# K and V loaded as 8 KB rows on every fourth partition, in the forward and backward pass of one decode step

## The chip, the cores and the metric

The kernel runs on one core of a Trainium2 chip. The metric is device time in microseconds (us) for one execution; lower is better. Before the change three runs took 282.91, 283.11 and 283.65 us; the median is 283.11 us.

## The reference, cut to what matters

One token of each of four sequences (B = 4, model width D = 512) goes through a layer norm and then through two branches side by side: attention with a cache of keys and values (32 query heads, 8 key/value heads, head width Dh = 128) and a gated feed-forward network (F = 1792). The kernel returns the output and the gradients of all inputs but `B_x`.

```python
W = min(4096, max(256, Sk // 4))                  # 1024 of the 4096 cached positions
q = (xn @ wq).reshape(B, 1, 32, 128)...
k = repeat(k_cache[:, :, Sk - W:, :], 4, axis=1)  # v likewise
p = softmax(q @ k^T * Dh**-0.5);  o = p @ v
out = x + o @ wo + (gelu(xn @ w_gate) * (xn @ w_up)) @ w_down
# and jax.vjp of it: gradients of x, k_cache, v_cache, wq, wo, w_gate, w_up, w_down
```

The gradients of the caches have the caches' full shape, (4, 8, 4096, 128) in bf16. Their first 3072 positions are zeros, and these zeros have to be written: 50 MB of the 81 MB that the kernel writes.

## The kernel before, in words

**Order of the work.** First the feed-forward branch (to about 60 us), then the query and its incoming gradient, then one round of the attention loop for each sequence `b`, then the end: `dwo` and `dwq`, the gradients of the two projection matrices.

**Loads of K and V.** `load_kv` (the issue is L233) fetches one sequence's K or V, 2 MB, into a tile `[128, G, J, Dh]` with J = 8: partition p holds the eight positions 8p to 8p + 7 of every head, so one row is 8 x 128 x 2 bytes = 2 KB. It issues two transfers of 1 MB, for four heads each. The first K load goes through SP's queue (q1 of the profile), the other seven loads through Pool's (q0). K has two tiles in turn, `ka` and `kb`; V has one, `va`, so V of the next sequence is issued only when `odq(0, b)` has read the present one, and K of the sequence after the next when `odq(1, b)` has read its tile.

**One round of the loop.** `scores(0, b)` is Q K^T and `scores(1, b)` is dO V^T, where dO is the gradient that comes into the attention's output. In both, DVE turns the tile in 32 x 32 blocks of bf16 pairs (`t32`, L93, four instructions of 1024 pairs), and PE multiplies what it wrote with `bd`, the query or dO spread out over blocks (`sc_ps`, 32 matmuls a call). `softmax` makes `E_f`, its sum, `P_b` (bf16) and `P_f` (fp32). `turned` brings `P_b` with its keys onto the partitions: 32 matmuls of 32 columns with the selector `selp` into `pT_ps`, and one eviction, `pT`. `odq(0, b)` multiplies `pT` with V. `dvdk(0, b)` makes the gradient of V: PE writes `kv_ps`, ACT and DVE evict it (L88, L89) into two of the four `stg` buffers of 1 MB, and two transfers (L106) store them. `softmax_d` makes `dS_b`, which goes the same way through `turned`, `odq(1, b)` and `dvdk(1, b)`.

**Queues.** SP's queue is in program order and carries the 32 stores of zeros, 1.5 MB each, with at most three in flight. Most are held by a load or a result: two or three follow the landing of each V or K load. Pool's queue carries the loads of K and V and the stores of results. A scheduler that goes by its own estimate of times puts the instructions of PE, DVE, ACT and Pool in order; loads have high priority. On each engine instructions then run strictly in that order. In the kernel before, the scheduler puts `va` of the third sequence, `kb` of the fourth and `va` of the fourth on Pool each ahead of one or two stores whose data are ready sooner.

Of the kernel before, what the change touches and what calls it, by code (L numbers as in the profile page):

```python
# [8 lines left out]
ACT = mybir.ActivationFunctionType  # L9
ALU = mybir.AluOpType  # L10
AX = mybir.AxisListType
FP32 = mybir.dt.float32
# [6 lines left out]
def kernel(  # L19
# [84 lines left out]
    def store(eng, out, in_, kind, apart, **kw):  # L104

        d = eng.dma_start(out=out, in_=in_, **kw)  # L106
        for k in apart:
            tc.declare_no_dep(d.ins, group=k, reason="stores write disjoint parts of the outputs")
        tc.add_to_no_dep_group(kind, d.ins)
        return d  # L110

    def result(out, in_):
        return store(nc.gpsimd, out, in_, "rest", ["zeros", "rest"], single_packet=True)

# [45 lines left out]
    def mask(name, n, in_):  # L160
# [9 lines left out]
    hm = mask("hm", Q, ident_f[:].rearrange("p (h d) -> p h d", d=4))  # L170
    omt = const.tile([P, NQ, 2], FP32, name="omt")
    TT(out=omt[:], in0=gmask[:].rearrange("p (c g) -> p c g", g=2), in1=bm[:].unsqueeze(2).broadcast_to([P, NQ, 2]),
       op=ALU.mult)
    om = mask("om", 2, omt[:].rearrange("p c g -> p g c"))
    oms = const.tile([P, 2], FP32, name="oms")
    TS(out=oms[:], in0=om[:], scalar1=scale, scalar2=None, op0=ALU.mult)
    gmask_b = const.tile([P, G], BF16, name="gmask_b")
# [34 lines left out]
    t32(dyP, pairs(dy_b[:]), 256)  # L212
    dyBD = const.tile([P, NPB, 2, P], BF16, name="dyBD")
    nc.gpsimd.memset(dyBD[:], 0.0)
    dyPb = dyP.bitcast(BF16).rearrange("p n (x r) -> p n r x", r=2)
# [11 lines left out]
    def load_kv(b, k, pool, tag, eng, **kw):  # L227
        d_, src = ((k_t, A_k_cache), (v_t, A_v_cache))[k]
        tl = pool.tile([P, G, J, Dh], BF16, name=tag, tag=tag)
        for hf in range(2):  # L230
            hs = slice(hf * G // 2, (hf + 1) * G // 2)
            with tc.high_priority():
                d = eng.dma_start(out=tl[:, hs].rearrange("p g j d -> p g (j d)"),  # L233
                                  in_=src[b, hs, K0:Sk, :].rearrange("g (m j) d -> m g (j d)", j=J), **kw)
        d_[b] = tl
        return d
# [23 lines left out]
    if True:  # L260
# [85 lines left out]
        for wi, (wsb, dh, og) in enumerate(((wu_sb, dhu, out_7), (wg_sb, dhg, out_6))):  # L346
# [26 lines left out]
            for h in range(2):  # L373
                stg = stg_tile()
                for ci in range(2):
                    for a, q in enumerate(quad):
                        ps = bank("dwg_ps", "w", (P, FQ))
                        mm(ps[:], xn_b[q, 2 * h + ci:D:C], dh_f[q, :], pos=(Q * a, 0))
                        o_ = (ci * NQ + a) * FQ
                        evac(stg[:, o_:o_ + FQ], ps[:], FQ)  # L380
                result(dwg_v[h], stg[:, 0:2 * F])
        nc.vector.tensor_copy(out=dxf[:], in_=dxf_ps[:])
    ffn_open.__exit__(None, None, None)

    with tc.tile_pool(name="mid", bufs=1, reuse_waits="tile") as mid:
# [4 lines left out]
        with tc.tile_pool(name="att", bufs=1, reuse_waits="tile") as att:  # L390
            zeros(2, load_kv(0, 1, att, "va", nc.gpsimd, single_packet=True))
            zeros(3, load_kv(1, 0, att, "kb", nc.gpsimd, single_packet=True))


# [3 lines left out]
            for k in range(2):  # L398
                bd.append([])
                for u in range(2):  # L400
                    t_ = att.tile([P, DPB, NQ, 2, 2, Q], BF16, name=f"bd{k}{u}")
                    nc.gpsimd.memset(t_[:], 0.0)
                    bd[k].append(t_)
            selh = att.tile([P, P + 4], FP32, name="selh")
# [61 lines left out]
            def get_d(ps, u):  # L466
                l_ = dsc[:, 512:640] if u == 0 else dsc[:, 640:768]
                mm(ps[:].rearrange("p b d -> p (b d)"), l_, dM.rearrange("p b e k -> p (b e k)"))

            spread_rows(1, get_d)  # L470

# [9 lines left out]
            def scores(k, b):  # L481

                t_ = bd[k][b % 2]
                ps = bank("sc_ps", ("S", "dP")[k], (P, NJ))
                src = pairs((k_t, v_t)[k][b][:])
                for g2 in range(2):
                    for e in range(2):
                        sc = scratch()
                        t32(sc[:].rearrange("p (c j m) -> p c j m", c=NQ, j=J), src[:, g2:G:2, :, e * Q:(e + 1) * Q], 1024)
                        sb = sc[:].bitcast(BF16).rearrange("p (c n r) -> p c r n", c=NQ, r=2)  # L490
                        for r in range(2):
                            for c, q in enumerate(quad):
# [26 lines left out]
            def softmax(S):  # L519
# [17 lines left out]
                rr = small("rr")  # L537
                nc.vector.reciprocal(out=rr[:], in_=es_ps[:])
                P_b = att.tile([P, NJ], BF16, name="P_b", tag="P_b")
                nc.scalar.activation(out=P_b[:], in_=E_f[:], func=ACT.Copy, scale=rr[:, 0:1])  # L540
                P_f = att.tile([P, NJ], FP32, name="P_f", tag="P_f")
                p_done = nc.scalar.activation(out=P_f[:], in_=E_f[:], func=ACT.Copy, scale=rr[:, 0:1])
                load["act"] += 1400
                return P_f, P_b, p_done

            def softmax_d(P_f, dP):
# [11 lines left out]
                return dS_b  # L558

# [17 lines left out]
            def odq(k, b, pT):  # L577
# [45 lines left out]
            for b in range(B):  # L623
                S = scores(0, b)
                if b + 1 < B:
                    dP = scores(1, b)
                    refill(0, b + 1)
                    refill(1, b + 1)
                P_f, P_b, p_done = softmax(S)
# [10 lines left out]
                dvdk(0, b, spread(P_b, 0), rows[1])  # L640
                dS_b = softmax_d(P_f, dP)
                dST = turned(dS_b, 1)
                o_done = odq(1, b, dST)
# [134 lines left out]
```

## Time and profile before

| | |
|---|---|
| the profiled execution | 282.91 us, of which the span of the profile is 280.8 us |
| median of the runs | 283.11 us |
| PE, DVE, ACT, POOL busy | 67%, 58%, 44%, 21% of the span |
| moved by DMA | 112.2 MB at 400 GB/s on average |
| q1 (SP's queue) | 66.46 MB: zeros, weights, the first K |
| q0 (Pool's queue) | 45.35 MB: results 30.7 MB, K and V 14.7 MB |
| granted PE clock, mean | 0.58 of full speed |

A profile is of one execution. Busy shares are over the whole span, and what a stage waits for is read from that stage. In the names of groups, L117 is the helper that issues nearly all matmuls, so that tiles (`pT_ps`, `sc_ps`, `kv_ps`, `od_ps`) tell them apart. The DMA share is the mean busy share of the core's 16 DMA engines, and the modelled records can bring it a little over 1.

### The profile page before, as it was taken

What the parts mean: (1) busy time and instruction counts of PE and PEld (TensorE: products, weight loads), DVE (VectorE), ACT (ScalarE), POOL (GpSimd) and SP (SyncE); (2) the same over time, 40 slices, a digit from 0 to 9 for tenths busy, and PEclk for the clock granted to TensorE, in tenths of its full rate; (3) what the DMA queues carried; (4) which work ended last, traced back from release to release, by engine and by line L of the source; (5) the groups of instructions that cost most, each with busy time, mean ns of one, the idle gap of its engine ahead of it and who ended that gap; (6) DMA issues with size and microseconds to landing.
All of it is one profiled execution on the core that took longest, in us unless ns stands there. A gap on an engine that the chain in (4) does not pass through costs nothing.

```text
span 280.8 us, 4407 instructions
## 1 busy us (share of the span) xinstructions
PE 187.0 (67%) x1733; PEld 76.1 (27%) x1733; DVE 162.9 (58%) x309; ACT 124.3 (44%) x245; POOL 60.2 (21%) x135
## 2 busy tenths in 40 slices
PE   0318899859444899659956642963357998955870
PEld 0102354233122623224321321321034232511210
DVE  2879656898796525545128350474496104397870
ACT  1133764730100569634824402722441768445870
POOL 8500110169083314130040060020020020201110
PEclk9975955558955556655555555555555555685555
DMA  7999999999999999999999999999999999999995
GB/s 246 427 443 443 388 396 420 425 426 411 389 427 434 420 356 403 308 373 415 424 412 407 421 427 409 371 428 427 436 373 418 415 408 402 390 411 386 414 412 242
DMA packets 17027, 112.21 MB, mean 400 GB/s; under 512 B 1384, under 2 KB 1648, under 8 KB 11376
## 3 DMA queue, kind: packets, MB, share of 16 engines
q1 hardware_dynamic: 6688, 66.46, 57.0%
q0 software_dynamic: 10176, 45.35, 41.5%
q8 instruction: 13, 0.21, 0.3%
q10 hardware_dynamic: 144, 0.13, 0.1%
q14 instruction: 6, 0.05, 0.0%
HBM read 30.93 MB, written 81.01 MB: 399 GB/s over the span
## 4 chain that ended last, share of the span: by engine, by line
PE 25%; DMA 24%; DVE 13%; issue 4%; ACT 4%; POOL 1%; POOLq 0%; DVEq 0%; ACTq 0%
DMA out_dram<-stg 16%; PE kv_ps L117 9%; DVE scr L93 6%; DMA ka<-in_A_k_cache_dram 5%; PE sc_ps L117 3%; ACT stg L88 3%; DMA kb<-in_A_k_cache_dram 3%; PE od_ps L117 3%; PE ok_ps L117 2%; PE ob_ps L117 2%; DVE stg L89 2%; DVE wq_sb L93 2%; PE dxq_ps L117 2%; PE dwq_ps L117 1%; PE dwo_ps L117 1%
## 5 line engine op out<-in xcount | busy, mean ns | idle before, releaser
L88 ACT CAST stg<-kv_ps 128x512 bf16<-128x512 f32 x118 | 63.7, 606 | 56.1 <-DMA out_dram<-stg 28.1
L106 POOL DMA_DIRECT2D out_dram<-stg x30 | 19.7, 659 | 146.3 <-ACT stg L88 96.1
L117 PE MATMUL sc_ps<-scr,bd 128*32 128x256 bf16 x256 | 24.2, 395 | 21.2 <-DVE scr L93 17.9
L117 PE MATMUL kv_ps<-dm,spr 32*128 32x256 bf16 x128 | 28.8, 400 | 6.7 <-ACT stg L88 5.1
L117 PE MATMUL kv_ps<-qm,spr 32*128 32x256 bf16 x128 | 24.9, 385 | 11.0 <-ACT stg L88 10.5
L93 DVE STREAM_TRANSPOSE scr<-va 128x1024 uint32<-128x1024 uint32 x16 | 18.8, 1217 | 10.9 <-DMA va<-in_A_v_cache_dram 10.9
L117 PEld LDWEIGHTS <-spr 32*128 32x128 bf16 x256 | 12.3, 102 | 46.3 <-issue 42.0
L117 PEld LDWEIGHTS <-bd 128*32 128x32 bf16 x256 | 8.1, 107 | 33.4 <-issue 32.7
L88 ACT CAST stg<-dwg_ps 128x448 bf16<-128x448 f32 x26 | 12.7, 552 | 6.7 <-PE dwg_ps L117 5.8
L88 ACT CAST stg<-dwo_ps 128x512 bf16<-128x512 f32 x18 | 10.0, 588 | 10.1 <-PE dwo_ps L117 9.9
L117 PE MATMUL dwo_ps<-dy_b,oSP 32*128 32x512 bf16 x32 | 9.0, 516 | 6.6 <-ACT stg L88 5.2
L89 DVE CAST stg<-kv_ps 128x512 bf16<-128x512 f32 x10 | 6.6, 679 | 11.8 <-DMA out_dram<-stg 6.3
L93 DVE STREAM_TRANSPOSE scr<-ka 128x1024 uint32<-128x1024 uint32 x8 | 9.6, 1227 | 5.4 <-DMA ka<-in_A_k_cache_dram 3.3
L93 DVE STREAM_TRANSPOSE scr<-kb 128x1024 uint32<-128x1024 uint32 x8 | 9.8, 1232 | 5.0 <-DMA kb<-in_A_k_cache_dram 4.4
L233 POOL DMA_DIRECT2D va<-in_A_v_cache_dram x8 | 6.0, 756 | 30.9 <-PE od_ps L117 27.1
L588 DVE SCALAR_TENSOR_TENSOR odt<-od_ps,oms,odt 128x128 f32<-128x128 f32 x4 | 1.4, 340 | 18.0 <-ACT odt L587 18.0
L117 PE MATMUL do_ps<-scr,dyBD 128*128 128x512 bf16 x32 | 10.1, 454 | 2.3 <-DVE scr L93 2.1
L117 PE MATMUL dwq_ps<-dqSP,xn_b 32*128 32x512 bf16 x32 | 10.6, 587 | 1.1 <-ACT stg L88 0.4
L89 DVE CAST stg<-dwq_ps 128x512 bf16<-128x512 f32 x15 | 9.9, 688 | 1.8 <-PE dwq_ps L117 1.6
L117 PEld LDWEIGHTS <-pT 128*32 128x32 bf16 x256 | 9.2, 140 | 5.2 <-ACT pT L88 2.3
L88 ACT CAST stg<-dwq_ps 128x512 bf16<-128x512 f32 x17 | 9.6, 586 | 1.6 <-PE dwq_ps L117 0.9
L89 DVE CAST stg<-dwo_ps 128x512 bf16<-128x512 f32 x14 | 9.2, 679 | 1.9 <-PE dwo_ps L117 1.6
(196 smaller groups left out, 321.1 us busy)
## 6 DMA issues: line engine op xcount, KB each, us to landing
out_dram<-ztile SPq DMA_DIRECT2D x32, 1536.0 KB, 12.2
out_dram<-stg POOLq DMA_DIRECT2D x24, 1024.0 KB, 10.7
va<-in_A_v_cache_dram POOLq DMA_DIRECT2D x8, 1024.0 KB, 15.0
out_dram<-stg POOLq DMA_DIRECT2D x6, 896.0 KB, 10.8
wq_sb<-in_A_wq_dram SPq DMA_DIRECT2D x1, 4096.0 KB, 24.0
wo_sb<-in_A_wo_dram SPq DMA_DIRECT2D x1, 4096.0 KB, 34.2
kb<-in_A_k_cache_dram POOLq DMA_DIRECT2D x4, 1024.0 KB, 19.4
ka<-in_A_k_cache_dram SPq DMA_DIRECT2D x2, 1024.0 KB, 42.2
```

The lines of the kernel that those rows point to most:

```text
L88: return nc.scalar.copy(out=out, in_=in_)
L89: return nc.vector.tensor_copy(out=out, in_=in_)
L93: nc.vector.transpose(out=out, in_=in_)
L106: d = eng.dma_start(out=out, in_=in_, **kw)
L117: nc.tensor.matmul(out, lhsT=lhsT, rhs=rhs, start=first, stop=last, **kw)
L233: d = eng.dma_start(out=tl[:, hs].rearrange("p g j d -> p g (j d)"), in_=src[b, hs, K0:Sk, :].rearrange("g (m j) d -> m g (j d)", j=J), **kw)
L588: done = STT(out=t_[:], in0=ps[:, 1, :], scalar=mk[:, 1:2], in1=t_[:], op0=ALU.mult, op1=ALU.add)
```

## The change

- **Rows.** K and V tiles become `[128, 2, Q, Dh]` with Q = 32. Partition 4m + c holds, for the two heads 2c and 2c + 1, the 32 positions 32m to 32m + 31: rows of 32 x 128 x 2 bytes = 8 KB. Each load is four transfers of 512 KB, one for each c, each to 32 partitions with a step of four.
- **Order on Pool.** Every transfer on Pool's queue is made to follow the one before it in program order (`in_order`). The last store of `dwg` is written after the first V and second K loads, where the scheduler had it already.
- **Scores.** The block transposes read one head of a pair and write their output in adjacent places. PE then reads every fourth pair for each c (`h j m c r` as `c r j m h`), 256 columns a matmul as before, neighbouring columns 1 KB apart.
- **turned.** Since one partition now serves only one pair of heads, the probabilities are laid out four times (`P_r`, 1024 columns, ACT; for the second call from `dS_b`), PE takes 128 matmuls of 32 columns in place of 32, and two DVE products with the mask `pmask` (512 columns each) take the place of one eviction of 256.
- **odq.** As many matmuls of the same size as before; the masks `om`, `oms` become `g2m`, `g2ms`.
- **Space.** The two `bd` tiles of dO (`bd10`, `bd11`) are put into `dyBD`, which Pool clears again after its last use; `pT` has one buffer in place of two.

```diff
+    def in_order(d):
+        if pool_dma:
+            tc.add_manual_dep(d.ins, pool_dma[-1].ins.name, ... NoSync ...)
+        pool_dma.append(d)
...
     def load_kv(b, k, pool, tag, eng, **kw):
-        tl = pool.tile([P, G, J, Dh], BF16, name=tag, tag=tag)
-        for hf in range(2):
-            hs = slice(hf * G // 2, (hf + 1) * G // 2)
+        tl = pool.tile([P, 2, Q, Dh], BF16, name=tag, tag=tag)
+        row = tl[:].ap[0][0]
+        for c in range(NQ):
             with tc.high_priority():
-                d = eng.dma_start(out=tl[:, hs].rearrange("p g j d -> p g (j d)"),
-                                  in_=src[b, hs, K0:Sk, :].rearrange("g (m j) d -> m g (j d)", j=J), **kw)
+                d = eng.dma_start(out=bass.AP(tensor=tl.tensor, offset=tl.offset + c * row,
+                                              ap=[[NQ * row, Q], [Q * Dh, 2], [1, Q * Dh]]),
+                                  in_=src[b, 2 * c:2 * c + 2, K0:Sk, :].rearrange("g (m j) d -> m g (j d)", j=Q), **kw)
+            if eng is nc.gpsimd:
+                in_order(d)
...
+            nc.gpsimd.memset(dyBD_t[:], 0.0)
             spread_rows(1, get_d)
...
-                        t32(sc[:].rearrange("p (c j m) -> p c j m", c=NQ, j=J), src[:, g2:G:2, :, e * Q:(e + 1) * Q], 1024)
-                        sb = sc[:].bitcast(BF16).rearrange("p (c n r) -> p c r n", c=NQ, r=2)
+                        t32(sc[:].rearrange("p (j x) -> p j x", j=Q), src[:, g2, :, e * Q:(e + 1) * Q], 1024)
+                        sb = sc[:].bitcast(BF16).rearrange("p (h j m c r) -> p c r j m h", h=4, j=J, m=8, c=NQ)
...
-            def turned(src, k):
-                ps = bank("pT_ps", "x", (P, J, Q))
-                for j in range(J):
-                    for a, q in enumerate(quad):
-                        mm(ps[q, j, :], src[:, j * Q:(j + 1) * Q], selp[:, a].rearrange("p c r -> p (c r)"), pos=(0, Q * a))
-                pT = att.tile([P, J, Q], BF16, name="pT", tag=f"pT{k}")
-                evac(pT[:], ps[:], NJ)
+            def turned(src):
+                pT = att.tile([P, Q, NQ, 8], BF16, name="pT", tag="pT")
+                for h in range(2):
+                    ps = bank("pT_ps", "x", (P, 16, Q))
+                    for j in range(16):
+                        o_ = (16 * h + j) * 8
+                        l_ = src[:, o_ * NQ:(o_ + 8) * NQ]
+                        for a, q in enumerate(quad):
+                            mm(ps[q, j, :], l_, selp[:, a].rearrange("p c r -> p (c r)"), pos=(0, Q * a))
+                    load["dve"] += 700
+                    TT(out=pT[:, 16 * h:16 * h + 16], in0=ps[:].rearrange("p j (c r) -> p j c r", c=NQ),
+                       in1=pmask[:].unsqueeze(1).unsqueeze(3).broadcast_to([P, 16, NQ, 8]), op=ALU.mult)
                 return pT
...
+                P_r = att.tile([P, NQ * NJ], BF16, name="P_r", tag="P_r")
+                nc.scalar.activation(out=fourfold(P_r), in_=by_part(E_f), func=ACT.Copy, scale=rr[:, 0:1])
                 P_b = att.tile([P, NJ], BF16, name="P_b", tag="P_b")
...
+                dS_r = att.tile([P, NQ * NJ], BF16, name="P_r", tag="P_r")
+                nc.scalar.copy(out=fourfold(dS_r), in_=by_part(dS_b))
...
                 for j in range(J):
-                    for c, q in enumerate(quad):
-                        mm(ps[q].rearrange("p g d -> p (g d)"), pT[:, j, :], src[:, 2 * c:2 * c + 2, j, :],
-                           j == 0, j == J - 1, (0, Q * c))
-                mk = (om, oms)[k]
+                    for a, q in enumerate(quad):
+                        mm(ps[q].rearrange("p g d -> p (g d)"), pT[:, 4 * j + a].rearrange("p c r -> p (c r)"),
+                           src[:, :, 4 * j + a, :], j == 0, j == J - 1, (0, Q * a))
+                mk = (g2m, g2ms)[k]
...
-                pT = turned(P_b, 0)
+                pT = turned(P_r)
...
-                dST = turned(dS_b, 1)
+                dST = turned(dS_r)
```

The built programs differ on the engines like this. PE has 768 more pairs of weight load and matmul (96 more in each of the eight calls of `turned`). Pool's queue reads, from the second V load on: V, two stores, K, two stores, V, two stores, K, two stores, V, and the remaining stores; before it read V, store, K, two stores, V, store, K, two stores, V, and the remaining stores. On DVE the transposes of the next K tile, which stood in the middle of a round, now follow the last step of that round's `odq(1, b)`, and the eight transposes of `wq` now stand ahead of the evictions that wait for a free `stg`.

More of the change, by code (lines that the diff above doesn't have):

```diff
@@ L110, in store @@
         return d
+    pool_dma = []
+    def in_order(d):
+        if pool_dma:
+            tc.add_manual_dep(d.ins, pool_dma[-1].ins.name,
+                              mybir.DependencyInfo(mybir.DependencyClass.NoSync, mybir.DependencyReason.DATA))
+        pool_dma.append(d)
     def result(out, in_):
-        return store(nc.gpsimd, out, in_, "rest", ["zeros", "rest"], single_packet=True)
+        in_order(store(nc.gpsimd, out, in_, "rest", ["zeros", "rest"], single_packet=True))
     def mm(out, lhsT, rhs, first=True, last=True, pos=None):
@@ L170 @@
     hm = mask("hm", Q, ident_f[:].rearrange("p (h d) -> p h d", d=4))
[L171 to L176, printed above, removed]
+    pmask = mask("pmask", NQ, ident_f[:].rearrange("p (m q) -> p q m", q=NQ))
+    g2ms = const.tile([P, 2], FP32, name="g2ms")
+    TS(out=g2ms[:], in0=g2m[:], scalar1=scale, scalar2=None, op0=ALU.mult)
     gmask_b = const.tile([P, G], BF16, name="gmask_b")
@@ L212 @@
     t32(dyP, pairs(dy_b[:]), 256)
-    dyBD = const.tile([P, NPB, 2, P], BF16, name="dyBD")
-    nc.gpsimd.memset(dyBD[:], 0.0)
+    dyBD_t = const.tile([P, NPB * 2 * P], BF16, name="dyBD")
+    nc.gpsimd.memset(dyBD_t[:], 0.0)
+    dyBD = dyBD_t[:].rearrange("p (n r m) -> p n r m", n=NPB, r=2)
     dyPb = dyP.bitcast(BF16).rearrange("p n (x r) -> p n r x", r=2)
@@ L380 @@
                         evac(stg[:, o_:o_ + FQ], ps[:], FQ)
-                result(dwg_v[h], stg[:, 0:2 * F])
+                if wi == 0 or h == 0:
+                    result(dwg_v[h], stg[:, 0:2 * F])
+        last_dw = (dwg_v[1], stg[:, 0:2 * F])
         nc.vector.tensor_copy(out=dxf[:], in_=dxf_ps[:])
@@ L392 @@
             zeros(3, load_kv(1, 0, att, "kb", nc.gpsimd, single_packet=True))
+            result(*last_dw)
             D3 = [att.tile([P, B, DPB, Q], U32, name=n) for n in ("D3q", "D3d")]
@@ L400 @@
                 for u in range(2):
-                    t_ = att.tile([P, DPB, NQ, 2, 2, Q], BF16, name=f"bd{k}{u}")
-                    nc.gpsimd.memset(t_[:], 0.0)
-                    bd[k].append(t_)
+                    if k == 0:
+                        t_ = att.tile([P, DPB * NQ * 4 * Q], BF16, name=f"bd{u}")[:]
+                        nc.gpsimd.memset(t_, 0.0)
+                    else:
+                        t_ = dyBD_t[:, u * 1024:(u + 1) * 1024]
+                    bd[k].append(t_.rearrange("p (e c g r m) -> p e c g r m", e=DPB, c=NQ, g=2, r=2))
             selh = att.tile([P, P + 4], FP32, name="selh")
@@ L468, in get_d @@
                 mm(ps[:].rearrange("p b d -> p (b d)"), l_, dM.rearrange("p b e k -> p (b e k)"))
+            nc.gpsimd.memset(dyBD_t[:], 0.0)
             spread_rows(1, get_d)
@@ L504, in spread, with fourfold, by_part @@
                 return sp
-            def turned(src, k):
-                ps = bank("pT_ps", "x", (P, J, Q))
-                for j in range(J):
-                    for a, q in enumerate(quad):
-                        mm(ps[q, j, :], src[:, j * Q:(j + 1) * Q], selp[:, a].rearrange("p c r -> p (c r)"), pos=(0, Q * a))
-                pT = att.tile([P, J, Q], BF16, name="pT", tag=f"pT{k}")
-                evac(pT[:], ps[:], NJ)
+            def fourfold(t_):
+                return t_[:].rearrange("p (h x c) -> p h x c", h=4, c=NQ)
+            def by_part(t_):
+                return t_[:].rearrange("p (x h) -> p h x", h=4).unsqueeze(3).broadcast_to([P, 4, 64, NQ])
+            def turned(src):
[10 more added lines that the diff above has]
+                       in1=pmask[:].unsqueeze(1).unsqueeze(3).broadcast_to([P, 16, NQ, 8]), op=ALU.mult)
                 return pT
@@ L542, in softmax @@
                 p_done = nc.scalar.activation(out=P_f[:], in_=E_f[:], func=ACT.Copy, scale=rr[:, 0:1])
-                load["act"] += 1400
-                return P_f, P_b, p_done
+                load["act"] += 2000
+                return P_f, P_b, P_r, p_done
             def softmax_d(P_f, dP):
@@ L556, in softmax_d @@
                 STT(out=dS_b[:], in0=dP, scalar=cc[:, 0:1], in1=P_f[:], op0=ALU.subtract, op1=ALU.mult)
+                dS_r = att.tile([P, NQ * NJ], BF16, name="P_r", tag="P_r")
+                nc.scalar.copy(out=fourfold(dS_r), in_=by_part(dS_b))
                 load["dve"] += 1200
-                return dS_b
+                load["act"] += 1200
+                return dS_b, dS_r
             def dvdk(k, b, sp, r_):
@@ L628 @@
                     refill(1, b + 1)
-                P_f, P_b, p_done = softmax(S)
+                P_f, P_b, P_r, p_done = softmax(S)
                 if b == B - 1:
@@ L640 @@
                 dvdk(0, b, spread(P_b, 0), rows[1])
-                dS_b = softmax_d(P_f, dP)
-                dST = turned(dS_b, 1)
+                dS_b, dS_r = softmax_d(P_f, dP)
+                dST = turned(dS_r)
                 o_done = odq(1, b, dST)
```

## The prediction, made before the changed kernel ran

> **What bounds the kernel now.** I read the slices of the span first. The DMA engines are busy in all of them, and no other engine is; PE has half its clock for most of the time.
>
> ```profile
> PE   0318899859444899659956642963357998955870
> DVE  2879656898796525545128350474496104397870
> DMA  7999999999999999999999999999999999999995
> GB/s 246 427 443 443 388 396 420 425 426 411 389 427 434 420 356 403 308 373 415 424 412 407 421 427 409 371 428 427 436 373 418 415 408 402 390 411 386 414 412 242
> ```
>
> The reader is to see that the DMA row hardly moves while the GB/s row does: busy engines move 308 to 443 GB/s, depending on what is in flight. So I asked the DMA view for stretches with one kind of traffic. From 70 to 75 us only V and K loads run, in 2 KB rows, taken two to a 4 KB packet; from 264 to 272 us only stores of 8 KB rows; from 88 to 95 us only zeros, 12 KB rows:
>
> ```profile
> DMA packets 498, 1.94 MB, mean 388 GB/s; under 512 B 25, under 2 KB 25, under 8 KB 497
> ...
> q0 software_dynamic: 496, 1.93, 101.9%
> ```
> ```profile
> DMA packets 450, 3.29 MB, mean 412 GB/s; under 512 B 48, under 2 KB 48, under 8 KB 48
> ...
> q0 software_dynamic: 450, 3.29, 100.3%
> ```
> ```profile
> DMA packets 272, 3.00 MB, mean 429 GB/s; under 512 B 28, under 2 KB 28, under 8 KB 28
> ```
>
> 388, 412 and 429 GB/s, each with full engines: time goes with packets as well as bytes. The trace's packet records agree: a 4 KB packet of a load takes 172 ns there, a 7 KB packet 272 ns, an 8 KB packet 309 at best and 319 on average, a 12 KB packet 460.
>
> Next, who shares. From 188 to 198 us zeros and stores are both queued, and the queues take packets one for one:
>
> ```profile
> q1 hardware_dynamic: 289, 3.16, 74.2%
> q0 software_dynamic: 286, 1.10, 27.0%
> ```
>
> With 4 KB against 12 KB, Pool's queue gets a quarter of the bandwidth. Last, the chain of waits, and what Pool waits for:
>
> ```profile
> 110.42 14.17 DMA ka<-in_A_k_cache_dram
> ...
> 141.77 7.43 DMA kb<-in_A_k_cache_dram
> ...
> 164.34 36.19 DMA out_dram<-stg
> ```
> ```profile
> POOL va L233 <- PE od_ps L117: 27.1, 3, 17.3
> POOL kb L233 <- PE od_ps L117: 15.8, 1, 15.8
> ```
>
> Compute stands still for these 58 us because its data are behind other transfers. Pool holds finished stores behind a load that waits for `od_ps`: the evictions of one pair end at 156 us, its stores are issued at 163.6, after `va` at 162.1. All packet times together, over 16 engines, are about 277 us of the 280.8. The bound is DMA time; compute counts where it leaves the DMA engines without work.
>
> **The change, part by part.**
>
> *K and V packets.* Pool's seven loads are 14.7 MB, 3584 packets of 4 KB. Over all of them the records have 176 ns on average, 631 us of one engine; at the 172.7 ns of the undisturbed stretch, 619. They become 1792 packets of 8 KB. No row shows an 8 KB load into every fourth partition. Nearest are the 7 KB rows of the weights (272 ns, scaled 311) and the 8 KB stores (309 to 320). Best end: 1792 x 309 = 554, (631 - 554)/16 = 4.8 us saved. Other end, if a load goes at the pace of the slowest one in the trace (209 ns for 4 KB, 418 for 8 KB): 749, 7.4 us lost. I take loads against the weight rows, 1792 x 311 = 557: (619 - 557)/16 = 3.9 us saved. The first K on SP goes from 1024 packets of 84.3 ns to 256 of 311: 0.4 us. Sum -4.3 us. Twice as many transfers cost 14 x 16 completion packets of 9 ns over 16 engines, 0.1 us, and two more issues for each load (row: 0.53 us for a store of 128 rows), some 0.5 us on Pool before the last quarter; the other quarters are then in flight. The Trainium skill, "DMA: Bandwidth & Descriptors", section "Rules for kernel authors", speaks against this part: it asks for 128 partitions and at least 1 MiB in one transfer. Its fixed cost of about 2 us, if it lay open for the 14 added transfers, would make the sum +24 us, not -4; the stretch from 70 to 75 us, across the border of two loads, is at 101.9% and shows none of it.
>
> *Sharing.* At 8 KB against 12 KB a load gets 40% beside zeros, not 25%. Total DMA work is the same; loads land sooner and zeros later. I give it no microseconds.
>
> *Pool's order.* Held stores go out up to 8 us sooner and free `stg`; the loads behind them wait only for stores that are ready when `od_ps` is. No cost; the gain is a compute chain that is earlier, which hides the next items. If that cover is gone they count.
>
> *turned and odq, V side (before the next V load).* From these rows at 91 us:
>
> ```profile
> 91.30 0.51 ACT L540 ACTIVATE P_b<-E_f,rr 128x256 bf16<-128x256 f32 x1 [0.94 <-DVE rr L538]
> ...
> 91.86 0.41 PE L117 MATMUL pT_ps<-selp,P_b 128*32 128x32 bf16 x32
> ...
> 92.36 0.37 ACT L88 CAST pT<-pT_ps 128x256 bf16<-128x256 f32 x1 [0.16 <-PE pT_ps L117]
> ...
> 95.51 1.50 POOL L233 DMA_DIRECT2D va<-in_A_v_cache_dram  x2 [2.21 <-PE od_ps L117]
> ```
>
> `P_r`, 1024 columns: ACT takes 0.37 us for 256 and 0.59 for 512 columns, so 0.51 + 3 x 0.23 = 1.2 us (at most 4 x 0.51 = 2.0), 0.7 later than `P_b` was. 128 matmuls: 0.19 us is the latency of one, the other 31 took 0.22; four times as many is 1.1 to 1.2, 0.8 more. The mask products: nearest row, DVE's eviction of 512 columns from PSUM, 0.68 us; the first lies beside the second half of the matmuls, the second follows it, 0.3 more than the old `pT`, and what DVE has ahead of it (`spr` 0.84, `Gt` 0.5) can add 0 to 1.3. Together 1.8 to 3.1; I take 2.2 us. All Pool transfers behind this load wait as long. *K side:* copying `dS_b` 1.0, matmuls 0.8, products 0.3 to 1.0: about 2.5 us, before the next K load.
>
> What lies beside them: in the first round the five zeros issued from 74.7 us end at about 100 us, and `va`'s packets begin 2.6 us after its issue, at 98.1. With loads 1 us quicker the zeros end at 99; with the issue at 97.7 the packets begin at 100.3 to 101. So the DMA engines stand 1.8 us (bounds 0 to 4). In the later rounds, after each such issue, two zeros (7.4 us) and two stores (5.2 us) are queued, over twice the 2.5 us. At the end the zeros that run until 263 us cover it.
>
> *Scores.* As many transposes (1.2 us) and matmuls. One transpose allows 8 matmuls, 0.62 us. No row has PE reading at 1 KB steps; bounds are 0.62 and, if each column cost four times as much, 0.19 + 4 x 0.43 = 1.9 us for eight. Up to a little over 1.1 us, DVE's pace hides all but the last eight. I take no cost. The Trainium skill, "SBUF — State Buffer", section "Door 1: The DMA port swizzle", states a penalty for each access to a new 16-byte line; by it PE would go towards the slow bound.
>
> *Rest.* Clearing `dyBD` (1.8 us on Pool) lies between the last `do_ps` matmul (72.8) and the first `sc_ps` (77.1), with the copies into `bd` behind it: 0 to 0.5 us, under the zeros. The masks cost nothing: as many small DVE operations as before.
>
> Sum against the profiled execution: 282.9 - 4.3 + 1.8 = **280.4 us** (its span 280.8 and 2.1 around it; it is 0.2 under the median of the runs).
>
> **The rivals.** *Engines leave the DMA idle, slower.* The longer way through `turned` lies ahead of every load. If both sides of two rounds stand open, where zeros run out, 2 x (2.2 + 2.5) = 9.4 comes on top: 282.9 - 4.3 + 9.4 = 288.0; all four rounds (which PE at quarter pace could do), 297 to 299. It decides from the point where an issue comes so late that zeros and stores in flight end before the load's packets begin. For it: the first round has hardly any margin, and PE works at half clock. Against: the DMA row has no slice under 9 in the loop, and 58 us of the chain are DMA waits.
>
> *Transfers to 32 partitions run slower, slower.* If a load kept only half of the 16 engines' pace, 16.8 MB would take 40 us more, some 318 us in all. Against: zeros are read from every second of 128 partitions and run at 429 GB/s. For: loads of this form are in no row.
>
> *The packets do not get cheaper.* If 8 KB loads cost what two 4 KB packets cost, only the 1.8 us stay: 284.
>
> *Order gains more.* Without the held stores the slow stretches (355 GB/s from 106 to 124 us) and the gaps at 104 and 252 us could go too, 2 to 4 us: 277.
>
> **How the numbers follow.** The measurement can tell about 0.3% (0.85 us) from no change. Forecast 280.4, own range 278.5 to 282.5: 0.49. Order gains more: 0.12. Packets no cheaper, 282.5 to 285: 0.13. Idle engines, 285 to 299, likeliest 288: 0.19. Half pace, 300 to 325: 0.07. Faster (under 282.3) holds nearly all of the first and the second, 0.58; the same (to 284.0) 0.12; slower half of the third and the last two, 0.30. From 276.5 to 290 leaves out the half pace, a quarter of the idle case and the edge of the second, some 0.15.
>
> **What would show it.** Right: in the records of Pool's queue 8 KB packets at 309 to 325 ns during loads; over 410 GB/s where loads run alone; no `va` wait over 17 us on Pool. The 1.8 us: a dip of the DMA row at 99 to 102 us. The idle case: DMA slices under 8 between 96 and 240 us, with `od_ps` ahead of a load in the chain. Half pace: load packets of 500 ns and more, or as many busy engines fewer. The forecast is wrong if the DMA row stays full and the sum of packet times does not fall by about 4 us, or if it falls and the span does not.

## The result, and the profile after

The changed kernel took 307.5 us (median of 6 runs, 306.9 to 309.2), the kernel before 283.0 us beside it (6 runs): a ratio of 1.087, with a 95% interval of 1.084 to 1.091. The forecast was 280.4 us, in a range of 276.5 to 290. The profiled execution is 306.9 us, its span 305.2, against 282.9 and 280.8 before. Ratios here leave out runs disturbed by a slower state of the chip, medians do not, so a ratio can differ a little from the quotient of two medians.

The slices of the span, the same rows as were shown of before:

```profile
PE   0428898785495993778848698114878964974860
DMA  7999999999998479999999999999449994998994
GB/s 267 432 464 412 365 424 432 421 420 427 427 431 345 171 287 396 368 395 392 371 405 426 357 421 372 374 433 430 174 184 411 425 384 175 404 385 347 411 375 178
```

Before, no slice of the DMA row inside the loop was under 9. Now it has holes: slices 14 and 15 (99 to 114 us, the first round), 29 and 30 (214 to 229 us) and 34 (252 to 259 us), where GB/s falls to 171 to 184 in the emptiest. In the packet records the sum of all packet times, over 16 engines, is 278.2 us (before 277.9), so the transfers cost what they did. The idle time of the DMA engines (the share of the 16 that had no packet under way, summed over the span) is 29.7 us against 6.6: 23.1 of the 24.4 us by which the span grew. The loss is idle DMA time, not slower DMA work.

Transfers to every fourth partition are not slow. The same stretch as before, 70 to 75 us, loads only:

```profile
DMA packets 328, 2.15 MB, mean 431 GB/s; under 512 B 65, under 2 KB 65, under 8 KB 65
...
q0 software_dynamic: 328, 2.15, 102.5%
```

431 GB/s against 388; a packet of 8 KB takes 309 to 310 ns there.

What opens the holes is in the chain of waits. Its shares of the span by engine, before and then after:

```profile
PE 25%; DMA 24%; DVE 13%; issue 4%; ACT 4%; POOL 1%; POOLq 0%; DVEq 0%; ACTq 0%
```
```profile
PE 41%; DVE 19%; ACT 15%; issue 11%; DMA 9%; SPq 1%; POOL 0%; POOLq 0%; DVEq 0%; ACTq 0%
```

DMA waits have shrunk, and "issue" has grown, time in which an engine waited for nothing that the profile shows. In the attention loop four long pieces of this kind stand on PE, and one DMA wait over 10 us is left:

```profile
97.87 1.76 issue
...
116.17 4.96 issue
...
141.02 12.97 DMA va<-in_A_v_cache_dram
...
191.01 4.68 issue
...
250.60 4.07 issue
```

On PE's timeline (start, busy time, in brackets the idle time before and what ended it) the first of them lies inside the burst of `turned`, the second behind one:

```profile
96.69 1.19 PE L126 MATMUL pT_ps<-selp,P_r 128*32 128x32 bf16 x117
99.63 0.25 PE L126 MATMUL pT_ps<-selp,P_r 128*32 128x32 bf16 x11 [1.76 <-issue]
```
```profile
115.78 0.39 PE L126 MATMUL kv_ps<-qm,spr 32*128 32x256 bf16 x1
121.13 0.36 PE L126 MATMUL kv_ps<-qm,spr 32*128 32x256 bf16 x1 [4.96 <-issue]
```

PE has six such waits from 96 us on (over 0.15 us each), 16.3 us in sum; before has none there. What PE waited for is found in another part of the page, the DMA queues. The queue that brings instructions, before and then after:

```profile
q8 instruction: 13, 0.21, 0.3%
```
```profile
q8 instruction: 19, 0.31, 0.4%
```

Each of these packets is 16 KB. The change adds 768 weight loads and 768 matmuls (2501 matmuls against 1733). Six packets more for 1536 instructions are 256 instructions to a packet; such a packet is called a piece below. And each of the four waits shown has the end of such a packet in it: packets begin at 97.27, 118.71, 193.33 and 252.33 us and take 0.9 to 1.0 us, and PE goes on 1.4 to 1.5 us after their ends. The places of the waits fit as well: counted in the order of their starts over all of PE's records, the number of instructions ahead of a wait leaves 193 or 194 when divided by 256, in all six. PE had run out of instructions, and the next piece came over the same 16 DMA engines. The Trainium skill, "Runtime: NRT & Kernel Launch", section "Instruction fetch mechanics", tells of blocks of 16 KiB with 256 instructions, which the trace bears out, and says that the cost of crossing from one to the next is mostly hidden; so it is in before from 96 us on, but in this trace it is up to 5.0 us where PE reached the border early.

Last, Pool at the start of the attention stage, where before issued its V and K loads and a store from 58.6 to 61.6 us without a wait:

```profile
58.91 2.16 POOL L240 DMA_DIRECT2D va<-in_A_v_cache_dram  x4 [3.83 <-DVE scr L93]
61.07 1.59 POOL L240 DMA_DIRECT2D kb<-in_A_k_cache_dram  x3
67.82 0.54 POOL L240 DMA_DIRECT2D kb<-in_A_k_cache_dram  x1 [5.16 <-DMA out_dram<-stg]
70.72 0.55 POOL L106 DMA_DIRECT2D out_dram<-stg  x1 [2.36 <-DMA va<-in_A_v_cache_dram]
71.26 1.86 POOL L416 MEMSET bd<- 128x1024 bf16 x2
```

The last quarter of K waits until an older store has landed, and the store behind it until the first quarter of V has. Counted along Pool's queue, each is the ninth transfer in flight and waits for the one eight places earlier. The limit is in the program: the instruction records show that Pool's transfers use eight semaphores in turn, and that each of these two issues waits for its own semaphore, which the transfer eight places earlier raises when it lands. Before never had more than six in flight. This wait is called Pool's hold below. The clearing of `bd` is queued behind, so it starts at 71.3 and not 62.2 us, and the first `sc_ps` matmul comes at 81.6 and not 77.1.

How the DMA share fell in two stretches of time (us, busy time of PE, PEld, DVE, ACT, POOL, granted clock, DMA share, GB/s), before and then after; the rounds of the changed kernel lie some us later, so the work in a stretch is not quite the same:

```profile
96.00:104.00 8.00, 7.84 (x71) 3.90 (x72) 2.17 (x8) 5.36 (x11) 1.92 (x6) 0.50 0.98 392
...
214.00:230.00 16.00, 15.52 (x117) 5.08 (x120) 2.89 (x12) 9.41 (x18) 1.11 (x2) 0.50 1.02 421
```
```profile
96.00:104.00 8.00, 6.22 (x188) 3.12 (x180) 5.02 (x11) 3.31 (x8) 2.82 (x8) 0.71 0.33 120
...
214.00:230.00 16.00, 12.53 (x209) 4.56 (x207) 11.49 (x23) 5.67 (x12) 1.50 (x2) 0.70 0.49 189
```

### The profile page after: what moved, and what is told of

Its sections match the earlier page's. It is cut to its first block, busy times and chain, and to the rows that moved or that the text cites. A ratio compares the mean times of both kernels' runs of the same rounds, so it can differ in the third digit from the quotient of the medians.

```text
span 305.2 us, 5999 instructions
## 1 busy us (share of the span) xinstructions
PE 200.4 (66%) x2501; PEld 75.3 (25%) x2501; DVE 172.5 (57%) x318; ACT 130.3 (43%) x251; POOL 65.4 (21%) x148
## 4 chain that ended last, share of the span: by engine, by line
PE 41%; DVE 19%; ACT 15%; issue 11%; DMA 9%; SPq 1%; POOL 0%; POOLq 0%; DVEq 0%; ACTq 0%
ACT stg L88 11%; PE sc_ps L126 8%; DVE scr L93 8%; PE kv_ps L126 7%; DMA va<-in_A_v_cache_dram 4%; DMA wu_sb<-in_B_w_up_dram 4%; PE od_ps L126 3%; PE dwg_ps L126 3%; PE dwo_ps L126 2%; PE do_ps L126 2%; PE ob_ps L126 2%; PE dwq_ps L126 2%; PE dxq_ps L126 2%; DVE dqs L636 2%; DMA out_dram<-stg 1%
## 5 line engine op out<-in xcount | busy, mean ns | idle before, releaser
L106 POOL DMA_DIRECT2D out_dram<-stg x30 | 19.9, 664 | 178.3 <-ACT stg L88 149.6
L126 PE MATMUL kv_ps<-qm,spr 32*128 32x256 bf16 x128 | 27.8, 395 | 6.9 <-issue 5.0
L126 PE MATMUL sc_ps<-scr,bd 128*32 128x256 bf16 x128 | 19.7, 636 | 17.3 <-DVE scr L93 17.2
L540 DVE TENSOR_TENSOR pT<-pT_ps,pmask 128x512 bf16<-128x512 f32 x16 | 10.5, 685 | 27.5 <-PE pT_ps L126 27.5
L126 PE MATMUL kv_ps<-dm,spr 32*128 32x256 bf16 x128 | 20.7, 327 | 1.6 <-ACT stg L88 0.3
L126 PE MATMUL sc_ps<-scr,dyBD 128*32 128x256 bf16 x128 | 18.3, 635 | 2.7 <-DVE scr L93 2.7
L126 PE MATMUL pT_ps<-selp,P_r 128*32 128x32 bf16 x1024 | 10.5, 192 | 6.8 <-ACT P_r L568 3.5
L126 PEld LDWEIGHTS <-dyBD 128*32 128x32 bf16 (+1 forms) x176 | 9.1, 103 | 22.4 <-issue 19.1
L240 POOL DMA_DIRECT2D va<-in_A_v_cache_dram x16 | 8.6, 543 | 25.9 <-PE kv_ps L126 13.0
L126 PEld LDWEIGHTS <-P_r 128*32 128x32 bf16 x1024 | 9.5, 100 | 10.8 <-ACT P_r L568 5.1
L126 PEld LDWEIGHTS <-bd 128*32 128x32 bf16 x128 | 4.0, 109 | 27.2 <-issue 25.1
## 6 DMA issues: line engine op xcount, KB each, us to landing
kb<-in_A_k_cache_dram POOLq DMA_DIRECT2D x8, 512.0 KB, 16.3
```

The costliest lines, as they stand in the source:

```text
L126: nc.tensor.matmul(out, lhsT=lhsT, rhs=rhs, start=first, stop=last, **kw)
L240: d = eng.dma_start(out=bass.AP(tensor=tl.tensor, offset=tl.offset + c * row, ap=[[NQ * row, Q], [Q * Dh, 2], [1, Q * Dh]]), in_=src[b, 2 ...
L540: TT(out=pT[:, 16 * h:16 * h + 16], in0=ps[:].rearrange("p j (c r) -> p j c r", c=NQ), in1=pmask[:].unsqueeze(1).unsqueeze(3).broadcast_to ...
```

## The experiments

Theory: three added costs make the loss, PE's waits for instructions, Pool's hold at the ninth transfer, and the fixed order, and 8 KB rows bring little against them. The rivals are those of the expectations. Times are medians; before, run beside each, lay at 282.6 to 283.0, and differences are taken from 283.0. e1_rows, e3_few, e6_few_near, e8_two and e9_rows_free return other values than the reference; only their time counts.

**e1_rows, e2_order, e3_few, e4_many: parts of the change, one by one.** e2_order is before with `in_order` on every Pool transfer and the late `last_dw` store. e1_rows adds the loads:

```
-        for hf in range(2):
...
+        for c in range(NQ):
...
+                d = eng.dma_start(out=bass.AP(tensor=tl.tensor, offset=tl.offset + c * row,
+                                              ap=[[NQ * row, Q], [Q * Dh, 2], [1, Q * Dh]]), ...
```

e3_few is the changed kernel with fewer matmuls in `turned`, e4_many the one before with more:

```
-                    for j in range(16):
+                    for j in range(0, 16, 4):
...
-                            mm(ps[q, j, :], l_, selp[:, a].rearrange("p c r -> p (c r)"), pos=(0, Q * a))
+                            mm(ps[q, j:j + 4, :], l_, selp[:, a].rearrange("p c r -> p (c r)").unsqueeze(1)
+                               .broadcast_to([P, 4, Q]), pos=(0, Q * a))
```
```
+                    for _ in range(4):
                         for a, q in enumerate(quad):
                             mm(ps[q, j, :], src[:, j * Q:(j + 1) * Q], ...
```

> The kernel before with the new loads (8 KB rows into every fourth partition, four transfers for each load) and Pool's fixed order, and nothing else: the computation reads the tiles in the old layout, so K and V stand in the wrong places and only the time counts. Theory (the DMA side did what was forecast, and the loss lies in what PE got to do): 8 KB packets at 309 to 325 ns, 278 to 280 us. Rival Pool (four issues a load hold Pool up, what stands behind them is late, and the fixed order adds to it): 287 us or more.

> The kernel before with Pool's fixed order alone; loads stay 2 KB rows in two transfers. Theory: order alone moves little, 281 to 283.5 us, the stores of the second and third round going out up to 8 us sooner. Rival Pool (the order itself costs): 286 us or more. Against the run with the rows as well it gives the price of the rows alone: 3 to 4 us less with rows by the theory.

> The changed kernel with 32 matmuls of 128 columns in each call of turned, in place of 128 matmuls of 32 columns (three of four positions get the weights of the first; the values are not those of the reference). It takes out the 768 added pairs of weight load and matmul and leaves P_r, the mask products, the 1 KB steps, the rows and the order. Theory (the bursts of small instructions outrun PE's supply of instructions: five waits of PE for nothing shown, 16.3 us): those waits gone, 288 to 292 us. Rivals (slow reads, Pool, or the longer chain): the waits stay or do not matter, 303 to 307 us.

> The kernel before with each matmul of turned issued four times over (same operands, same result): exactly the 768 added pairs, nothing else. Theory (bursts): waits of PE for nothing shown, 1.5 to 5 us each, right after the bursts, and 287 to 297 us, less than 16 us where the chain waits for DMA anyway. Rivals: 283 to 284.5 us, since 96 more matmuls at 7 ns are 0.7 us a call and lie under the DMA.

Measured: e2_order 286.6 us (ratio 1.016, 1.011 to 1.021), e1_rows 291.4 (1.030, 1.026 to 1.034), e3_few 291.3 (1.030, 1.027 to 1.033), e4_many 286.9 (1.014, 1.011 to 1.017).

The order alone costs 3.6 us (4.0 against the before that ran beside it), as the rival had it. Pool's timeline shows what it takes away; before, and then e2_order:

```profile
106.22 0.76 POOL L106 DMA_DIRECT2D out_dram<-stg  x1 [4.47 <-ACT stg L88]
109.68 1.49 POOL L233 DMA_DIRECT2D ka<-in_A_k_cache_dram  x2 [2.70 <-PE od_ps L117]
111.16 0.76 POOL L106 DMA_DIRECT2D out_dram<-stg  x1
```
```profile
105.11 0.76 POOL L106 DMA_DIRECT2D out_dram<-stg  x1 [4.47 <-ACT stg L88]
106.09 0.76 POOL L106 DMA_DIRECT2D out_dram<-stg  x1 [0.22 <-ACT pT L88]
108.57 1.50 POOL L242 DMA_DIRECT2D ka<-in_A_k_cache_dram  x2 [1.72 <-PE od_ps L126]
```

Issued at nearly the same time, the K load has one more store of 1 MB ahead of it. Its wait in the chain grows from 14.2 to 19.1 us; V lands 19.9 us after its issue, not 15.0, and K in `kb` 23.4, not 19.4 (medians). On balance it was better to hold the stores back: compute waits for each load, and though the chain of before has a wait of 36.2 us for a store too, letting the stores go first made the kernel slower.

e1_rows adds 4.8 us, with Pool's waits of 5.33 and 2.97 us at 62 to 71 us and three of 2.9 to 3.0 us in front of the next quarters of `kb`. e3_few has all of the change but the bursts, and is level with e1_rows, so that `P_r`, `dS_r`, the mask products and the strided reads seem to cost nothing there. But two effects can cancel: e1_rows has Pool's hold in its later rounds as well, from 127 to 174 us, and e3_few has there one such wait, of 1.5 us; the changed kernel has none after 71 us. From e3_few to the changed kernel the 96 more pairs to each `turned` cost 16.2 us, the sum of PE's waits (16.3). In e4_many the same number of pairs gave waits of 2.20 and 0.35 us only, and a time just under the expected 287 to 297; the bursts alone do not fix the price.

**e8_two, e9_rows_free: Pool's hold, and the rows by themselves.** The edit of the loads, in e8_two with the order, in e9_rows_free without:

```
+        for g2 in range(2):
...
+                d = eng.dma_start(out=bass.AP(tensor=tl.tensor, offset=tl.offset + g2 * Q * Dh, ap=[[row, P], [1, Q * Dh]]),
+                                  in_=src[b, g2:G:2, K0:Sk, :].rearrange("c (m j) d -> m c (j d)", j=Q), **kw)
```

> The kernel of e1_rows (before, with the 8 KB rows and the fixed order) with each load in two transfers, one for each group of a pair, to all 128 partitions, in place of four to 32 partitions. K and V stand in other places than the scores and products assume, as in e1_rows. Theory that Pool is held because four transfers to a load bring more than eight into flight: the 5.3 and 3.0 us waits of Pool at 67 to 71 us and the 2.9 us ones at 137 to 147 us are gone, and the time falls from e1_rows' 291.4 to the price of the order (286.6) less the cheaper packets (2.2 us): 284 to 286. Rival, that the 4.8 us come from 8 KB rows themselves (another share beside zeros, other landings) however many transfers bring them: 290 to 292.

> The kernel before with one edit alone: K and V in 8 KB rows, two transfers to 128 partitions for each load. No fixed order, nothing added on PE, ACT or DVE; K and V stand in other places than the scores and products assume. Theory (order 4 us, hold 4.8 us, packets 2.2 us and 0.4 us for the first K): 280 to 281, the only edit of the change that gains. Rival, that 8 KB rows delay zeros or stores as much as they save: 283 or more.

Measured: e8_two 287.9 us (1.018, 1.016 to 1.020), e9_rows_free 283.4 (1.002, 0.999 to 1.004). Two transfers in place of four take 3.5 us off e1_rows, and the hold is gone from Pool's timeline:

```profile
60.16 1.09 POOL L242 DMA_DIRECT2D kb<-in_A_k_cache_dram  x2
61.19 0.59 POOL L106 DMA_DIRECT2D out_dram<-stg  x1
61.72 3.70 POOL L416 MEMSET bd<- 128x1024 bf16 x4
```

The time is 2 us above what was expected, since the rows did not pay. e9_rows_free shows that by itself: the sum of packet times is 275.7 us, 2.2 less than before, and the idle time of the DMA engines is 9.7 us, 3.1 more. No time is won; the rival was nearer. From e9_rows_free to e8_two the fixed order costs 4.5 us, the second measure of it.

**e6_few_near: reads at 1 KB steps.** In `scores`, on e3_few:

```
-                        sb = sc[:].bitcast(BF16).rearrange("p (h j m c r) -> p c r j m h", h=4, j=J, m=8, c=NQ)
+                        sb = sc[:].bitcast(BF16).rearrange("p (c n r) -> p c r n", c=NQ, r=2)
```

> The kernel of e3_few (the changed kernel with 32 matmuls of 128 columns in turned) with PE reading the transposed K and V at 4-byte steps again, not at 1 KB steps: the columns of the scores stand in another order. Theory that the slower reads (636 ns for a score matmul against 396) lie beside DVE's transposes: the matmul is back at 390 to 450 ns and the time stays at e3_few's, 290 to 292.5. Rival, that the strided read paces the scores and so every load that waits for od_ps: 287 to 289.

Measured: 291.0 us (1.028, 1.026 to 1.030) against 291.3. One tile's instructions (shortest, median and longest ns), in e3_few and then in e6_few_near:

```profile
L126 PE MATMUL sc_ps<-scr,bd x128: 614/636/687, 80.8 to 200.9; 128*32 128x256 bf16 x128
```
```profile
L126 PE MATMUL sc_ps<-scr,bd x128: 372/406/421, 81.4 to 195.5; 128*32 128x256 bf16 x128
```

A matmul takes 636 ns with the steps and 406 without, and the time is the same: DVE's transposes at 1.23 us still pace the scores.

**e10_two_stage, e14_two_stage_zero, e18_two_stage_first, e15_zero: a kernel for the new rows without the bursts.** `turned` keeps the old 32 matmuls; four matmuls of 256 columns with 0/1 matrices `lh` then put each row of four keys on its four partitions:

```
+                p1 = att.tile([P, J, Q], BF16, name="p1", tag="p1")
+                evac(p1[:], ps[:], NJ)
...
+                        mm(ps[:, 8 * h:8 * h + 8, :].rearrange("p j x -> p (j x)"), lh[:, 2 * u + h, :],
+                           p1[:].rearrange("p j x -> p (j x)"))
```

e14_two_stage_zero issues one zeros transfer earlier, e15_zero does that to before, and e18_two_stage_first puts `turned` and `odq` of e14_two_stage_zero under `tc.high_priority()`:

```
-            zeros(3, load_kv(1, 0, att, "kb", nc.gpsimd, single_packet=True))
+            zeros(4, load_kv(1, 0, att, "kb", nc.gpsimd, single_packet=True))
...
-                    zeros((2, 2, 4)[b], ...
+                    zeros((2, 2, 3)[b], ...
```

> The whole reference, from the changed kernel: loads in two transfers, no fixed order, and turned in two stages: the 32 matmuls and the eviction of before, then four matmuls of 256 columns with a 0/1 matrix that puts a row of four keys onto each of its four partitions, then the two mask products. P_r, dS_r and the 128 pairs are gone. Theory: no issue waits on PE, no Pool wait for the transfer eight earlier; the path through turned is longer than before by the four matmuls (0.9 us) and the products (0.3 to 0.7), 1.5 us or so on each side, and the packets save 2.6: 280.5 to 283. Rival, that the longer path leaves the DMA engines idle in several rounds, as the idle case of the prediction has it: 286 to 290.

> The whole reference: e10_two_stage with one of the zeros transfers (1.5 MB, 3.7 us of DMA) issued with the second sequence's K in the first round, in place of the last va load. Theory that the longer path through turned costs mainly the 3.4 us in which the DMA engines stand at 97 to 107 us: the added transfer fills them, 285.5 to 287 against 288.8. Rival, that the loads of the first round wait behind the added zeros for as long as they fill, or that later rounds matter as much: 288 to 290.

> The whole reference: the kernel before with the same zeros transfer moved to the first round and nothing else, as a control for e14_two_stage_zero. Before has 0.7 us idle in the first round: 282.3 to 283.5 if only idle time counts; 284 to 286 if the loads of the first round lose what the zeros gain.

> The whole reference: e14_two_stage_zero with turned and the products od_ps at high priority, so that PE, ACT and DVE take them ahead of the kv_ps products of the pair before. Theory that the path from the probabilities to od_ps, which each load waits for, is what the correct kernel with 8 KB rows still loses: 283 to 285.5 against 286.3, near or under the kernel before. Rival, that the products held back delay their stores as much: 286 to 289.

Measured: e10_two_stage 288.8 us (1.019, 1.015 to 1.024), e14_two_stage_zero 286.3 (1.009, 1.006 to 1.012), e15_zero 284.3 (1.003, 1.001 to 1.006), e18_two_stage_first 284.8 (1.003, 0.998 to 1.007). No PE waits for instructions are left after 96 us. e10_two_stage is 5.4 us over e9_rows_free, in the rival's range: the longer way through `turned` is not free when Pool's order is left to the scheduler. (e10_two_stage has the strided reads too, which cost nothing in e3_few.) Its DMA share in the first round, by stretches:

```profile
96.00:104.00 8.00, 8.00 (x109) 3.36 (x99) 5.50 (x15) 6.07 (x13) 1.07 (x2) 0.78 0.88 341
104.00:116.00 12.00, 11.85 (x84) 3.61 (x80) 3.94 (x6) 7.52 (x17) 2.64 (x4) 0.58 0.79 312
```

In the first round the engines are idle for 3.5 us (97 to 99 and 104 to 107 us), before for 0.8. One more zeros transfer there takes 2.5 us off the median; the same in before, which had no hole to fill, opens one of 3.4 us at 204 to 208 us and costs 0.3%. With `turned` and `odq` first, the ratio cannot be told from 1, though the median is still 1.8 us over before's. So 8 KB rows can be had with no loss that these runs show, and none of the versions run is faster than before.

**e12_shift, e13_many_shift, e16_free_bursts, e17_order_many: what a burst costs, and where.** The first two put 64 small pairs, half a piece of instructions, early into the changed kernel and into e4_many:

```
     nc.vector.tensor_copy(out=xnT[:], in_=tps[:])
+    sh_ps = bank("sh_ps", "x", (P, Q))
+    for _ in range(64):
+        mm(sh_ps[0:Q, :], ident[:, 0:Q], ident[:, 0:Q], pos=(0, 0))
```

e16_free_bursts is the changed kernel with the two-transfer loads of e9_rows_free and no `in_order`; e17_order_many is e2_order with the edit of e4_many.

> The changed kernel with 64 small matmuls more (32 x 32, their output not used) right after the transposes of x, where PE waits for weights: half of a 16 KB piece of PE's instructions, so that all later pieces end 64 pairs elsewhere. Theory that PE stands after a burst when the piece runs out there and the next is only then asked for: the issue waits come at other bursts than those of the changed kernel (99.6, 121.1, 195.7, 254.7 us), none over 5.0 us, and their sum S is another than 16.3; the time is 291 + S, which for an S of 5 to 20 is 296 to 311. Rival, that the waits belong to these bursts and to what the DMA does then: the same four bursts, S 15 to 18, 306 to 309.

> The kernel of e4_many (before, with each matmul of turned issued four times, 128 pairs in a burst) and the same 64 small matmuls early. e4_many had only 2.6 us of issue waits on PE and 286.9 us. Theory of the pieces: 64 pairs further on more of the eight bursts run over the end of a piece, the waits add up to 5 us or more, and the time is 288 to 296. Rival, that the old kernel's order of work leaves the instruction queue time to run ahead: 1 to 3 us of waits, 286 to 288.5.

> The whole reference: the changed kernel with its loads in two transfers to 128 partitions and Pool's order left to the scheduler; P_r, the 128 pairs of turned and all else are kept. S is the sum of PE's issue waits in its trace. Theory that such a wait goes whole into the time only where a load waits behind it and the DMA queues have run dry, which the fixed order makes common: e10_two_stage's 288.8 (the same order of transfers without the bursts) plus less than half of S. Rival, that each microsecond of S is one of the time, as between the changed kernel, e12_shift and e3_few: 288.8 + S, with S of 5 to 16 some 294 to 305.

> The kernel before with Pool's transfers in the fixed order (e2_order, 286.6) and each matmul of turned issued four times (e4_many, 286.9). Theory that under the fixed order PE's issue waits S count one for one: 286.6 + S, and S of 4 to 12 makes 290 to 299. Rival, that the two costs only add as they were measured apart: 286.6 + 3.5, some 290 whatever S is.

Measured: e12_shift 300.4 us (1.062, 1.059 to 1.065), e13_many_shift 286.3 (1.010, 1.006 to 1.013), e16_free_bursts 295.7 (1.046, 1.041 to 1.050), e17_order_many 288.8 (1.021, 1.017 to 1.025). Adding 64 pairs of work to the changed kernel made it 7 us faster, as the theory of the pieces expected. Its waits are now at other places, none where they were:

```profile
132.79 1.25 PE L126 MATMUL od_ps<-va,pT 128*32 128x256 bf16 x18 [4.46 <-issue]
```
```profile
153.97 0.40 PE L126 MATMUL od_ps<-kb,pT 128*32 128x256 bf16 x2 [4.46 <-issue]
```

The six kernels with bursts have 21 such waits after 90 us, and in each the instructions ahead of it, divided by 256, leave 191 to 194: they stand at the ends of pieces and nowhere else. With S the sum of these waits, and the time of the nearest kernel without bursts:

| kernel | S, us | time, us | without bursts, us | difference, us |
|---|---|---|---|---|
| after | 16.3 | 307.5 | 291.3 (e3_few) | 16.2 |
| e12_shift | 9.4 | 300.4 | 291.3 (e3_few) | 9.1 |
| e16_free_bursts | 7.1 | 295.7 | 288.8 (e10_two_stage) | 6.9 |
| e17_order_many | 2.5 | 288.8 | 286.6 (e2_order) | 2.2 |
| e4_many | 2.6 | 286.9 | 283.0 (before) | 3.9 |
| e13_many_shift | 5.4 | 286.3 | 283.0 (before) | 3.3 |

S itself is a matter of where the pieces end. The theory that the order of Pool's transfers decides what a wait costs fell: with the order free, in e16_free_bursts, S still counts one for one. e17_order_many lies under both of its expectations, because its S is 2.5 us and not the 4 to 12 assumed. Only in before's own order of work do the two part, e4_many 1.3 us over its S and e13_many_shift 2.1 under (and under the 288 expected of it); why there, these runs do not settle.

## Why the prediction was wrong

From before to after, step by step: order +3.6 (e2_order), rows in two transfers +1.3 (e8_two), Pool's hold +3.5 (e1_rows), the other work of `turned` and the strided reads -0.1 (e3_few), bursts +16.2. The steps are measured in this order and do not add alike in another: without order and hold the longer path through `turned` is worth 5.4 us (e10_two_stage over e9_rows_free), with them nothing. That both delay the same loads of the first round is one reason that fits, the later holds of e1_rows, which e3_few lacks, another; no run separates the two.

- *128 matmuls, "0.8 more".* The term that failed. Its size as busy time is nearly right, 1.24 to 1.39 us where no wait lies inside, against the 1.1 to 1.2 forecast. But it priced them by the rate at which 31 of them had run from instructions already at hand, and did not ask for their supply: 256 instructions use up a whole piece in some 1.3 us, and PE then stood up to 5.0 us for the next. At the four waits shown, 4.7 to 7.7 us passed from PE's first instruction of one piece to its first of the next. No row of before shows such a wait, and its PE had no burst over 32 pairs in `turned`; the six-packet growth of the instruction queue could have been worked out, its price not.
- *Pool's order, "No cost".* Wrong by 3.6 to 4.5 us. The stores held for 8 us were read as a loss. The row that mattered was the load that went ahead of them.
- *Two more issues for each load, "some 0.5 us on Pool".* An issue is 0.53 to 0.54 us, as said. The step did not count what is in flight: the ninth waits for the landing of the one eight earlier, 5.16 and 2.36 us, with the clearing of `bd` behind it. It is worth 3.5 us between e8_two and e1_rows, where it comes back in later rounds; what the two waits at the start cost the changed kernel, no run shows by itself. The Trainium skill, "DMA: Bandwidth & Descriptors", section "Rules for kernel authors", which the prediction set against this part, asks for 128 partitions and at least 1 MiB in a transfer; e8_two bears it out in its time, though not by a slower transfer, since 32 partitions took 431 GB/s: the four transfers ran into the program's eight semaphores.
- *K and V packets, -4.3.* The price of an undisturbed packet, 311 ns, is right (309 to 310). Over all 1792 loads it is 333, beside stores and zeros, so 2.2 us were saved and not 3.9; the first K saved its 0.4. In the changed kernel zeros then cost 2.0 us more, 475 against 467 ns on average. And e9_rows_free shows the other error: 2.2 us less DMA work ended as 3.1 us more idle time. "The bound is DMA time" held only within those few microseconds.
- *`P_r`, `dS_r`, products.* 1.15 us against 1.2, 1.05 to 1.14 against 1.0, 0.685 against 0.68: right.
- *The 1.8 us in the first round, bounds 0 to 4.* Mis-sized. The engines are idle for 7.2 us between 98 and 111 us in the changed kernel, for 5.1 in e3_few, and in the first round for 3.5 in e10_two_stage, which has neither hold nor order nor bursts: the last is the nearest to what that step meant.
- *Sharing, no microseconds.* Right in the time, which is the same in e9_rows_free; but what was to land sooner hardly did. V lands 14.9 us after its issue, not 15.0, K in `kb` 18.1, not 19.4, and stores 13.5, not 10.7 (medians).
- *Strided reads, no cost.* Right, between its bounds: two blocks of 8 matmuls take 2.23 to 2.25 us, one 1.1, just DVE's pace.
- *The rivals.* The idle engines came, with the signs named for them (DMA slices under 8, `od_ps` ahead of loads); the prices were worked out from the length of `turned` alone, so even 297 to 299 was too low. Half pace and cheaper order did not come.

## What to carry to other kernels

A burst of short PE instructions can cost more than its busy time: count weight loads and matmuls against the 256 instructions of a 16 KB piece, and where PE runs through a piece in a few microseconds, price the border at up to 5 us, as it was here, or use fewer, wider matmuls. Full DMA engines are not a condition that these runs show: their share was 0.99 during the waits of 4.96 and 4.68 us, but 0.64 during that of 4.07. Before a transfer is split, count what its queue then has in flight against the semaphores that the program gives it, and before an order is fixed, ask which of two transfers somebody waits for. When DMA is full in every slice, look at how far behind it compute is: a saving of 1% in packet time came back as idle time of the DMA engines.

## What was not expected of the hardware

- PE stood 4.1 to 5.0 us for a piece of instructions, of which the transfer took 0.9 to 1.0; half a piece of useless work early moved the time of the whole kernel by 7 us.
- What looks like a limit of the DMA queue is the program's: in e1_rows and the changed kernel a transfer on Pool's queue that had eight ahead of it in flight waited until the eighth before it had landed (0.9 to 5.3 us), because the issue waits for the one of eight semaphores that the two share. Whether the chip would hold more in flight, no run tells.
- Loads of 8 KB rows ran at 431 GB/s into every fourth partition, as fast as into all 128 in e9_rows_free (428); averaged over the whole run, mostly beside stores and zeros, the same packets took 333 ns, 8% more than 309.
- PE's reads at 1 KB steps cost 636 ns for 256 columns against 406 at 4-byte steps, far less than four times.
